# First tile of a fused attention and two-layer MLP kernel: the clamp moves from VectorE to ScalarE, and every low half of the activation goes to VectorE

## The chip, the cores and the metric

One core of one Trainium2 chip runs the whole program. The metric is device time in microseconds (us) of one execution, and lower is better. The kernel before the change took 991.78 us (median of three runs, 990.30 to 991.88).

The engines have these names in the profile: PE is TensorE's matmul stream and PEld its weight loads, DVE is VectorE, ACT is ScalarE, POOL is GpSimd, SP is SyncE, which issues the DMAs. Each engine works through its own list of instructions in the listed order.

## The reference, cut to what matters

An attention with a decaying state (4 batches, 8 heads, 768 tokens, head size 48) gives 3072 rows of 384 values; two MLPs follow, each with an inner width of 2048. The change touches the activation of the first MLP:

```python
h = x @ w_in                       # 3072 x 384 times 384 x 2048
neg, pos = h <= -1, h >= 1
g = np.where(pos, h, np.where(neg, 0.0, (h + 1) ** 2 / 4))
x = g @ w_out                      # 2048 x 384
```

## The kernel before

The 3072 tokens are cut into 8 tiles of 384 (`TILES`). For each tile of the first MLP, `step(s)` runs over 16 slices `f` of 128 inner columns, so steps 0 to 15 are the first tile. Each product is made of three matmuls on values that are split in a high and a low half: `gemm1` (line 661) issues 9 matmuls into a PSUM tile `hp`, and `gemm2` (line 670) issues 9 into the three sums `acc`, three steps later in the program (`LAG = 3`). `hp` comes from a pool of two buffers (`ps_h`), so the `hp` of a step can start only when the last reader of the `hp` two steps before is done.

Between the two products stands the activation:

- `relu2_a`: DVE clamps `hp` to [-1, 1] (line 698), ACT squares with scale and bias (line 699).
- `relu2_b`: DVE takes the larger of that and `hp` (line 711); this is the last reader of `hp`. Then `high_g` lets ACT round it to the high half `gh` (line 692).
- `low_g` (line 686), one step later, makes the low half `gl` as the difference of the two. In the first tile the engine alternates by `LOW0`, 0 being POOL and 1 being DVE: seven of the fifteen that fall under `LOW0` are on POOL and eight on DVE. From step 16 on `LOW_E` decides.

Beside the first tile run two other streams. The weights of the first MLP arrive in 32 pieces as 64-bit numbers (`wst`, line 140, four buffers) and are converted: DVE shifts and masks (line 650, into `ct`) and merges (line 652), ACT converts the low word (line 651), POOL adds the two (line 654), ACT makes the high half `whi` (line 168), and DVE or POOL the low half `wlo` (line 177, even pieces on DVE, odd ones on POOL, from piece 10 on). The attention of the next tiles goes in windows of 128 tokens (`window`): scans on DVE (lines 433 and 435), a masked copy on DVE (line 489), the scores `sc` on PE (line 484), the split of the result into `xx` (lines 537 and 538), and loads of `rk` (line 400) that a scan waits for.

What sets the order: for steps 0 to 15 (`AUTO = 16`) a scheduler of the compiler places every instruction in its engine's list by a model of its own of the time; from step 16 on the order is that of the program (`manual_schedule`). So a change in the first tile can move anything in the lists up to step 16, and nothing behind it.

Of the kernel before, what the change touches and what calls it, by code (L numbers as in the profile page):

```python
# [9 lines left out]
F32 = mybir.dt.float32  # L10
# [3 lines left out]
AF = mybir.ActivationFunctionType  # L14
# [24 lines left out]
TN = 384  # L39
# [12 lines left out]
LO0 = 'p'  # L52
LO1 = 'dg'
PUT = 1
ALT = (0,)
ALT_N = 1
N0 = 10
PRIO = True
WTS = ('wt', 'gh', 'wt', 'gl', 'wt', 'ev')
WBS = ('wb', 't')  # L60
LOW0 = (0, 1)
XL_N = 6
F0 = 0
WP0 = 400
# [35 lines left out]
def fast_path(st, tc, rkw_t, nat, v_l, w1, w2, u, out, x2_d, w2_d, flag_i, force):  # L100
    nc = tc.nc
    one = st.enter_context(tc.tile_pool(name="one", bufs=1))
    p2 = st.enter_context(tc.tile_pool(name="p2", bufs=2))
# [80 lines left out]
    def conv_w1():  # L184
        new = to_f32(0, 2) if nconv[0] < NPC else []
        if nconv[0] <= N0:
            half.extend(new)
            new = []
        while half:
            split_w(*half.pop(0))  # L190
        half.extend(new)
# [6 lines left out]
    def add_w2():  # L198
        while puts:
            i, wf = puts.pop(0)  # L200
            nc.sync.dma_start(out=w2_d[:, i, :], in_=wf)
        while adds:
            i, t, b = adds.pop(0)
            nc.gpsimd.tensor_tensor(out=t, in0=t, in1=b, op=ALU.add)
            puts.append((i, t.bitcast(F32)))
# [3 lines left out]
    def low_w2(keep):  # L209
        while len(late) > keep:  # L210
            i, wf = late.pop(0)
            f, q = pieces[i]
            (nc.gpsimd, nc.vector)[i % 2].tensor_tensor(out=wlo[f][q], in0=wf, in1=whi[f][q].bitcast(F32), op=ALU.subtract)
            load_w(2)

    def fetch_w2():
        i = nconv[2]
        if i < NPC:
            nconv[2] += 1
            f, q = pieces[i]  # L220
            wf = staged.pop((2, i))
            nc.scalar.activation(out=whi[f][q], in_=wf, func=AF.Copy)
            late.append((i, wf))
# [11 lines left out]
    def where(s):  # L235
        if s < KF * len(TILES):
            return (0, s // KF, s % KF) + TILES[s // KF]
        s -= KF * len(TILES)
        return (1, s // KF, s % KF) + TILES2[s // KF]
# [15 lines left out]
    def evac(l, i, t0, n):  # L255
        acc = accs.pop((l, i))
        for j in range(KD if l == 0 else n // 128):
            c = n if l == 0 else DM
            ev = p2.tile([128, TN], F32, tag="ev", name="ev", bufs=3)
            if j == 1:  # L260
                nc.vector.tensor_copy(ev[:, 0:c], acc[j][:, 0:c])
            else:
                nc.scalar.activation(out=ev[:, 0:c], in_=acc[j][:, 0:c], func=AF.Copy)  # L263
            if l == 0:
                nc.sync.dma_start(out=x2_d[:, j, t0:t0 + n], in_=ev[:, 0:n])
            else:
                nc.sync.dma_start(out=out[t0 + 128 * j:t0 + 128 * (j + 1)], in_=ev[:, 0:DM])

    def step(s):
        if s < NS:  # L270
            l, i, f, t0, n = where(s)
            last = l == 0 and i == len(TILES) - 1
            slots = l == 0 and not last
            if l == 0 and f == 0:
                cur[0] = i
            if l == 0 and i == 0:
                with hooks["prio"](CP1):
                    while nconv[0] < min(NPC, 2 * f + 2 + AHEAD):
                        conv_w1()
                    if nconv[0] == NPC:  # L280
                        conv_w1()
            hp = pools["h"][s % len(pools["h"])].tile([128, 512], F32, tag="h", name="hp")
            gemm1(nc, hp, n, xh[l, i], xl[l, i], f, win, whi, wlo)
            if l == 0 and ALT[f % len(ALT)] and i < ALT_N:
                t = relu2_c(nc, p2, hp, n, (None, nc.gpsimd, nc.vector)[ALT[f % len(ALT)]])
            else:
                t = (relu2_a, swish_a)[l](nc, p2, hp, n)
        if s - 1 in gq:
            low_g((nc.gpsimd, nc.vector)[(LOW_E if s >= 16 else LOW0)[s % len(LOW_E)]], p2, gq, s - 1, where(s - 1)[4])
        if s < NS:  # L290
            if slots:
                per = KF - F0 if i == 0 else KF
                if i > 0 or f >= F0:
                    credit[0] += (TILES[i + 1][1] // W) * 8 * KF // per
                if credit[0] >= KF:
                    credit[0] -= KF
                    hooks["attn"]()

        if s >= LAG:
            pl, pi, pf, pt0, pn = where(s - LAG)  # L300
            if pf == 0:
                accs[pl, pi] = [ps_a.tile([128, 512], F32, tag=f"acc{j}", name=f"acc{j}") for j in range(KD if pl == 0 else pn // 128)]
            if pl == 0:
                gemm2(nc, accs[pl, pi], pn, gq.pop(s - LAG), pf, wout, whi, wlo)
            else:
                gemm3(nc, accs[pl, pi], gq.pop(s - LAG), pf, wout, whi, wlo)
            if pf == KF - 1:
                evac(pl, pi, pt0, pn)
            if pl == 0 and pi == len(TILES) - 1:
                low_w2(0)  # L310
                while nconv[2] < 2 * (pf + 1):
                    fetch_w2()
                if pf == KF - 1:
                    low_w2(0)
        if s < NS:
            gq[s] = (relu2_b, swish_b)[l](nc, p2, t, hp, n)
        if s < NS:
            if l == 0 and i >= 1:
                if i == 1 and f == 0:
                    for _ in range(WST):  # L320
                        load_w(1)
                add_w2()
                if f in PRE_F and nconv[1] < NPC:
                    conv_w2()
            if slots:
                while credit[0] >= KF:
                    credit[0] -= KF
                    hooks["attn"]()
            if last and f == 0:
                for _ in range(WS2):  # L330
                    load_w(2)
                load_x2(0)
            if last and f == 8:
                split_x2(0)
            if l == 1 and CHECK_LATE:
                if i == 0 and f == 0:
                    for _ in range(WCK):
                        load_w(3)
                if f % 2 and nconv[3] < NPC:
                    c = nconv[3]  # L340
                    nconv[3] += 1
                    check_w(0, c, staged.pop((3, c))[:, :, 1].bitcast(I32), AF.Sigmoid)
                    load_w(3)
            if l == 1 and i + 1 < len(TILES2):
                if f == 4:
                    load_x2(i + 1)
                if f == 12:
                    split_x2(i + 1)
# [308 lines left out]
def gemm1(nc, hp, n, xh, xl, f, win, whi, wlo):  # L657
    i = 0
    for a, b in ((whi, xh), (whi, xl), (wlo, xh)):
        for kk in range(KD):  # L660
            nc.tensor.matmul(out=hp[:, 0:n], lhsT=win(a, f, kk), rhs=b[:, kk, 0:n], start=(i == 0), stop=(i == 3 * KD - 1))  # L661
            i += 1


def gemm2(nc, acc, n, g, f, wout, whi, wlo):
    gh, gl = g
    for j in range(KD):
        i = 0
        for a, b in ((whi, gh), (whi, gl), (wlo, gh)):
            nc.tensor.matmul(out=acc[j][:, 0:n], lhsT=wout(a, f, j * 128, 128), rhs=b[:, 0:n], start=(f == 0 and i == 0), stop=(f == KF - 1 and i == 2))  # L670
            i += 1


def gemm3(nc, acc, g, f, wout, whi, wlo):
    gh, gl = g
    for j, o in enumerate(acc):
        i = 0
        for a, b in ((gh, whi), (gl, whi), (gh, wlo)):
            nc.tensor.matmul(out=o[:, 0:DM], lhsT=a[:, j * 128:(j + 1) * 128], rhs=wout(b, f, 0, DM), start=(f == 0 and i == 0), stop=(f == KF - 1 and i == 2))  # L679
            i += 1  # L680


def low_g(eng, p2, gq, f, n):
    t, gh, _ = gq[f]
    gl = p2.tile([128, TN], F32R, tag="gl", name="gl", bufs=3)
    eng.tensor_tensor(out=gl[:, 0:n], in0=t[:, 0:n], in1=gh[:, 0:n].bitcast(F32), op=ALU.subtract)  # L686
    gq[f] = gh, gl
# [15 lines left out]
def relu2_c(nc, p2, hp, n, eng):  # L703
    t = p2.tile([128, TN], F32, tag="t", name="t", bufs=3)
    nc.scalar.activation(out=t[:, 0:n], in_=hp[:, 0:n], func=AF.Relu, bias=0.5, scale=0.5)
    eng.scalar_tensor_tensor(out=t[:, 0:n], in0=t[:, 0:n], scalar=1.0, in1=t[:, 0:n], op0=ALU.min, op1=ALU.mult)
    return t


def relu2_b(nc, p2, t, hp, n):  # L710
    nc.vector.tensor_tensor(out=t[:, 0:n], in0=t[:, 0:n], in1=hp[:, 0:n], op=ALU.max)  # L711
    return high_g(nc, p2, t, n)
# [163 lines left out]
```

## Time and profile before

| what | before |
|---|---|
| time, median of 3 runs | 991.78 us |
| profiled execution, its own time | 991.68 us |
| span of the profiled execution | 990.0 us |
| PE busy, share of the span | 944.4 us, 95% |
| DVE busy | 580.2 us, 59% |
| ACT busy | 528.0 us, 53% |
| POOL busy | 389.5 us, 39% |
| chain that ended last, PE's share | 80% |

The shares are means over stages that differ. The attention and the conversion of weights fill the first 120 us, with DVE and POOL near their limit and PE with gaps; after that PE has no gaps. What a change in the first tile is worth is read in that first stretch.

### The profile page before, as it was taken

To read this page: it belongs to the slowest core of one execution; us is meant where nothing else is said; L and a number is where in the kernel's file an instruction comes from. 1 tells how busy PE (TensorE), PEld (TensorE's weight loads), DVE (VectorE), ACT (ScalarE), POOL (GpSimd) and SP (SyncE) were. 2 spreads that over 40 slices of the span, in tenths; PEclk is the share of its full clock that TensorE was granted. 3 is DMA by queue.
4 is the path that set the end of the run, shared out by engine and by line. 5 is a ranking of instruction groups with operands and counts; after the bars stand their busy time and mean duration, and the time that the engine had idled before them with its cause. 6 is when DMAs were issued, how large, how long until landed. Compare 5 with 4: busy or idle time off the path is not lost.

```text
span 990.0 us, 18582 instructions
## 1 busy us (share of the span) xinstructions
PE 944.4 (95%) x6976; PEld 906.6 (92%) x6976; DVE 580.2 (59%) x1001; ACT 528.0 (53%) x1255; POOL 389.5 (39%) x398
## 2 busy tenths in 40 slices
PE   4757999999999999999999999999999999999997
PEld 2446899999999999999999999999999999999997
DVE  6889977887878778788755743232323323232321
ACT  4666555666756667665654565545454433333332
POOL 6788744555555646447423431111111111111111
PEclk9978999999999999999999999999999999999999
DMA  9876534544645445464204442323232101010000
GB/s 240 217 206 168 164 104 112 136 112 140 183 116 155 120 130 162 118 168 105 72 17 145 128 153 57 110 64 113 65 112 65 48 1 48 1 46 4 25 1 29
DMA packets 54531, 102.90 MB, mean 104 GB/s; under 512 B 8608, under 2 KB 33696, under 8 KB 54432
## 3 DMA queue, kind: packets, MB, share of 16 engines
q1 hardware_dynamic: 54432, 101.63, 36.0%
q8 instruction: 57, 0.93, 0.4%
q14 instruction: 42, 0.34, 0.1%
HBM read 83.51 MB, written 15.73 MB: 100 GB/s over the span
## 4 chain that ended last, share of the span: by engine, by line
PE 80%; DVE 7%; DMA 4%; issue 3%; ACT 3%; POOL 1%; SPq 0%; DVEq 0%; ACTq 0%; POOLq 0%
PE hp L661 37%; PE acc L679 20%; PE acc L670 18%; DMA rk<-rkw_t 2%; PE yt L515 2%; PE kv L509 2%; PE sc L484 2%; DMA wst<-w 1%; DVE pi L433 1%; DVE rk L441 1%; DVE t L711 1%; DVE t L698 1%; DVE wlo L177 1%; DVE ct L650 1%; PE tp L479 0%
## 5 line engine op out<-in xcount | busy, mean ns | idle before, releaser
L661 PE MATMUL hp<-xx,whi 128*128 128x384 f32 x1536 | 318.0, 342 | 7.4 <-DVE t L711 5.2
L686 POOL TENSOR_TENSOR gl<-t,gh 128x384 fp32r<-128x384 f32 x128 | 136.9, 1070 | 471.3 <-ACT gh L692 443.6
L661 PEld LDWEIGHTS hp<-xx,whi 128*128 128x128 f32 x1536 | 273.2, 190 | 9.8 <-DVE t L711 5.7
L692 ACT ACTIVATE gh<-t 128x384 fp32r<-128x384 f32 x256 | 134.1, 524 | 194.8 <-DVE t L711 116.8
L722 DVE TENSOR_TENSOR t<-t,hp 128x384 f32<-128x384 f32 x128 | 70.8, 553 | 218.7 <-ACT t L717 218.2
L661 PE MATMUL hp<-xx,wlo 128*128 128x384 f32 x768 | 177.6, 340 | 0.0
L717 ACT ACTIVATE t<-hp 128x384 f32<-128x384 f32 x128 | 62.9, 491 | 145.9 <-PE hp L661 145.8
L661 PEld LDWEIGHTS hp<-xx,wlo 128*128 128x128 f32 x768 | 139.0, 189 | 0.0
L670 PE MATMUL acc<-gh,whi 128*128 128x384 f32 x384 | 130.2, 350 | 0.7 <-ACT ev L263 0.6
L670 PE MATMUL acc<-gl,whi 128*128 128x384 f32 x384 | 130.3, 339 | 0.3 <-POOL gl L686 0.3
L679 PE MATMUL acc<-wlo,gh 128*128 128x384 f32 x384 | 130.2, 339 | 0.0
L679 PE MATMUL acc<-whi,gh 128*128 128x384 f32 x384 | 129.9, 338 | 0.0
L670 PE MATMUL acc<-gh,wlo 128*128 128x384 f32 x384 | 129.6, 337 | 0.0
L679 PE MATMUL acc<-whi,gl 128*128 128x384 f32 x384 | 129.3, 337 | 0.0
L686 DVE TENSOR_TENSOR gl<-t,gh 128x384 fp32r<-128x384 f32 x128 | 80.8, 631 | 51.1 <-ACT gh L692 49.7
L699 ACT ACTIVATE t<-t 128x384 f32<-128x384 f32 x128 | 66.5, 519 | 70.9 <-DVE t L698 70.5
L711 DVE TENSOR_TENSOR t<-t,hp 128x384 f32<-128x384 f32 x128 | 70.1, 548 | 30.5 <-ACT t L699 28.7
L698 DVE TENSOR_SCALAR t<-hp 128x384 f32<-128x384 f32 x128 | 70.3, 549 | 29.3 <-PE hp L661 29.1
L670 PEld LDWEIGHTS acc<-gh,whi 128*128 128x128 f32 x384 | 72.4, 190 | 3.6 <-ACT ev L263 1.3
L670 PEld LDWEIGHTS acc<-gl,whi 128*128 128x128 f32 x384 | 72.2, 188 | 0.7 <-POOL gl L686 0.5
L670 PEld LDWEIGHTS acc<-gh,wlo 128*128 128x128 f32 x384 | 72.1, 188 | 0.0
L679 PEld LDWEIGHTS acc<-whi,gl 128*128 128x128 f32 x384 | 72.1, 188 | 0.0
(98 smaller groups left out, 1278.9 us busy)
## 6 DMA issues: line engine op xcount, KB each, us to landing
wst<-w SPq DMA_DIRECT2D x96, 384.0 KB, 3.6
rk<-rkw_t SPq DMA_DIRECT2D x48, 288.9 KB, 6.1
rkn<-nat SPq DMA_DIRECT2D x24, 384.0 KB, 4.5
lt<-v_l SPq DMA_DIRECT2D x48, 128.0 KB, 3.0
w_d<-wt SPq DMA_DIRECT2D x32, 192.0 KB, 4.6
w2f<-w_d SPq DMA_DIRECT2D x32, 192.0 KB, 2.5
vn<-nat SPq DMA_DIRECT2D x24, 192.0 KB, 2.7
x_d<-ev SPq DMA_DIRECT2D x24, 192.0 KB, 4.2
```

The lines of the kernel that those rows point to most:

```text
L484: nc.tensor.matmul(out=sc[64 * (1 - hh):64 * (1 - hh) + 64, mc, :], lhsT=kt[p, mc, :], rhs=rt[p, mc, :], start=True, stop=True)
L509: nc.tensor.matmul(out=kv[c][64 * hh:64 * hh + D, m, :], lhsT=kn_t[q, m, 64 * hh:64 * hh + D], rhs=vn[q, m, hh, :], start=True, stop=True)
L661: nc.tensor.matmul(out=hp[:, 0:n], lhsT=win(a, f, kk), rhs=b[:, kk, 0:n], start=(i == 0), stop=(i == 3 * KD - 1))
L670: nc.tensor.matmul(out=acc[j][:, 0:n], lhsT=wout(a, f, j * 128, 128), rhs=b[:, 0:n], start=(f == 0 and i == 0), stop=(f == KF - 1 and i == 2))
L679: nc.tensor.matmul(out=o[:, 0:DM], lhsT=a[:, j * 128:(j + 1) * 128], rhs=wout(b, f, 0, DM), start=(f == 0 and i == 0), stop=(f == KF - 1 a ...
L686: eng.tensor_tensor(out=gl[:, 0:n], in0=t[:, 0:n], in1=gh[:, 0:n].bitcast(F32), op=ALU.subtract)
L692: nc.scalar.activation(out=gh[:, 0:n], in_=t[:, 0:n], func=AF.Copy)
L698: nc.vector.tensor_scalar(t[:, 0:n], hp[:, 0:n], scalar1=-1.0, scalar2=1.0, op0=ALU.max, op1=ALU.min)
L699: nc.scalar.activation(out=t[:, 0:n], in_=t[:, 0:n], func=AF.Square, bias=0.5, scale=0.5)
L711: nc.vector.tensor_tensor(out=t[:, 0:n], in0=t[:, 0:n], in1=hp[:, 0:n], op=ALU.max)
L717: nc.scalar.activation(out=t[:, 0:n], in_=hp[:, 0:n], func=AF.Sigmoid, scale=1.702)
L722: nc.vector.tensor_tensor(out=t[:, 0:n], in0=t[:, 0:n], in1=hp[:, 0:n], op=ALU.mult)
```

## The change

Two settings change. `ALT = (1,)` sends all 16 steps of the first tile through a new function, `relu2_d`, in place of `relu2_a`: ACT makes the clamp by two relus, out of PSUM and then in place, and squares in a third instruction. `LOW0 = (1, 1)` puts `gl` on DVE in every step of the first tile.

```diff
-ALT = (0,)
+ALT = (1,)
...
-LOW0 = (0, 1)
+LOW0 = (1, 1)
...
             if l == 0 and ALT[f % len(ALT)] and i < ALT_N:
-                t = relu2_c(nc, p2, hp, n, (None, nc.gpsimd, nc.vector)[ALT[f % len(ALT)]])
+                t = relu2_d(nc, p2, hp, n)
             else:
                 t = (relu2_a, swish_a)[l](nc, p2, hp, n)
...
+def relu2_d(nc, p2, hp, n):
+    t = p2.tile([128, TN], F32, tag="t", name="t", bufs=3)
+    nc.scalar.activation(out=t[:, 0:n], in_=hp[:, 0:n], func=AF.Relu, bias=0.5, scale=-0.5)
+    nc.scalar.activation(out=t[:, 0:n], in_=t[:, 0:n], func=AF.Relu, bias=1.0, scale=-1.0)
+    nc.scalar.activation(out=t[:, 0:n], in_=t[:, 0:n], func=AF.Square)
+    return t
```

In the changed file the two relus and the square are lines 712, 713 and 714, and the maximum is line 719 (711 before).

The scheduler then sets the lists anew. Up to the row ahead of the first clamp all of DVE's rows are as before. DVE's list just around the seventh maximum, the one that frees the `hp` buffer for step 8 (step `f` has the low half `wlo_0_` with the number 110 + 2f, so 132 belongs to slice 11). Before:

```order
L177 TENSOR_TENSOR wlo_0_132<-wt,whi_0_100 128x384
L652 SCALAR_TENSOR_TENSOR wt<-wst,ct 128x384
L698 TENSOR_SCALAR t<-hp 128x384
L434 RECIPROCAL seed<-pi 128x4
L650 TENSOR_SCALAR ct<-wst 128x384
L435 SCALAR_TENSOR_TENSOR pi<-rk_164,seed 128x516
L652 SCALAR_TENSOR_TENSOR wt<-wst,ct 128x384
L711 TENSOR_TENSOR t<-t,hp 128x384
L698 TENSOR_SCALAR t<-hp 128x384
```

and with the change:

```order
L177 TENSOR_TENSOR wlo_0_136<-wt,whi_0_104 128x384
L652 SCALAR_TENSOR_TENSOR wt<-wst,ct 128x384
L686 TENSOR_TENSOR gl<-t,gh 128x384
L650 TENSOR_SCALAR ct<-wst 128x384
L177 TENSOR_TENSOR wlo_0_138<-wt,whi_0_106 128x384
L652 SCALAR_TENSOR_TENSOR wt<-wst,ct 128x384
L650 TENSOR_SCALAR ct<-wst 128x384
L719 TENSOR_TENSOR t<-t,hp 128x384
L652 SCALAR_TENSOR_TENSOR wt<-wst,ct 128x384
L177 TENSOR_TENSOR wlo_0_140<-wt,whi_0_108 128x384
```

The same maximum now stands behind the low halves of slices 12, 13 and 14 (134, 136, 138), which came after it before.

PE's list where the scores `sc` begin of the last window that falls in the first tile. Before, from the end of the second product of step 6 on (`whi_0_96` is slice 9, `whi_1_91` slice 6):

```order
L670 MATMUL acc_932<-gl,whi_1_91 128x384
L670 MATMUL acc_932<-gh,wlo_1_123 128x384
L484 MATMUL sc<-rk_163 64x64 x5
L661 MATMUL hp<-xx,whi_0_96 128x384 x6
L661 MATMUL hp<-xx,wlo_0_128 128x384 x3
L670 MATMUL acc_930<-gh,whi_1_93 128x384
```

and with the change, from the end of the second product of step 3 on (`whi_0_90` is slice 6, `whi_1_85` slice 3):

```order
L670 MATMUL acc_936<-gl,whi_1_85 128x384
L670 MATMUL acc_936<-gh,wlo_1_117 128x384
L484 MATMUL sc<-rk_163 64x64 x16
L661 MATMUL hp<-xx,whi_0_90 128x384 x6
L661 MATMUL hp<-xx,wlo_0_122 128x384 x3
L670 MATMUL acc_934<-gh,whi_1_87 128x384
```

The scores of that window stood in three parts behind step 8 before; now they stand ahead of step 6. Everything else that PE has done when it comes to step 8 is the same in both lists. At step 12 they have done the same work altogether, and from step 17 on they agree row by row.

## Rows read from the trace of the kernel before

**Rows 1.** The page's 40 slices of the span: PE's busy tenths and its granted clock.
```profile
PE   4757999999999999999999999999999999999997
...
PEclk9978999999999999999999999999999999999999
```

**Rows 2.** Busy time by stretch: stretch, length, PE, PEld, DVE, ACT, POOL, clock, DMA share, GB/s.
```profile
79.40:116.60 37.20, 31.74 (x259) 27.72 (x255) 35.26 (x58) 21.93 (x50) 30.27 (x30) 0.86 0.57 152
116.68:144.12 27.44, 27.44 (x167) 26.48 (x168) 22.66 (x40) 16.86 (x37) 15.66 (x15) 0.94 0.51 136
144.12:990.00 845.88, 838.00 (x6066) 820.10 (x6065) 457.79 (x797) 442.94 (x1061) 284.35 (x286) 1.00 0.31 90
```

**Rows 3.** What PE's matmuls waited for, 117 us to the end (total, times, longest).
```profile
PE hp L661 <- DVE t L711: 1.8, 1, 1.8
PE acc L670 <- ACT ev L263: 0.6, 2, 0.4
PE fp L642 <- DVE st L640: 0.3, 1, 0.3
```

**Rows 4.** The chain that ended last, 110 to 150 us: start, length, what.
```profile
116.16 0.47 DVE t L711
...
116.68 3.18 PE hp L661 x9
...
121.66 0.49 PE sc L484 x10
...
124.46 0.60 PE sc L484 x14
...
128.43 0.38 PE sc L484 x8
```

**Rows 5.** DVE's groups, 79.4 to 134 us: busy, mean ns, idle before and releaser.
```profile
L177 DVE TENSOR_TENSOR wlo<-wt,whi 128x384 fp32r<-128x384 f32 x8 | 8.1, 1017 | 0.0
L650 DVE TENSOR_SCALAR ct<-wst 128x384 int32<-128x384 int32 x14 | 7.6, 546 | 0.0
...
L686 DVE TENSOR_TENSOR gl<-t,gh 128x384 fp32r<-128x384 f32 x6 | 7.5, 1255 | 0.0
L698 DVE TENSOR_SCALAR t<-hp 128x384 f32<-128x384 f32 x12 | 6.5, 544 | 0.2 <-PE hp L661 0.2
...
L489 DVE COPY_PREDICATED ra<-mask,sc 64x512 f32<-64x512 int32 x6 | 4.4, 742 | 0.2
L433 DVE TENSOR_TENSOR_SCAN pi<-rk,one_s 128x516 f32<-128x516 f32 x2 | 2.8, 1407 | 1.6 <-DMA rk<-rkw_t 1.6
...
L538 DVE TENSOR_TENSOR xx<-yt,xx 128x512 fp32r<-128x512 f32 x2 | 1.3, 666 | 0.0
```

**Rows 6.** DVE's timeline, single instructions: start, length, what.
```profile
79.47 0.54 DVE L698 TENSOR_SCALAR t<-hp 128x384 f32<-128x384 f32 x1
...
107.52 2.35 DVE L686 TENSOR_TENSOR gl<-t,gh 128x384 fp32r<-128x384 f32 x1
...
116.09 0.54 DVE L711 TENSOR_TENSOR t<-t,hp 128x384 f32<-128x384 f32 x1
116.55 0.54 DVE L698 TENSOR_SCALAR t<-hp 128x384 f32<-128x384 f32 x1
...
117.48 0.54 DVE L686 TENSOR_TENSOR gl<-t,gh 128x384 fp32r<-128x384 f32 x1
```

**Rows 7.** POOL's timeline beside two of those instructions.
```profile
107.48 1.00 POOL L654 TENSOR_TENSOR wt<-wt,wb 128x384 int32<-128x384 int32 x1
108.45 1.01 POOL L686 TENSOR_TENSOR gl<-t,gh 128x384 fp32r<-128x384 f32 x1
...
116.47 1.01 POOL L654 TENSOR_TENSOR wt<-wt,wb 128x384 int32<-128x384 int32 x1
```

**Rows 8.** ACT's groups: a PSUM read (the page) and the square (79.4 to 134 us).
```profile
L717 ACT ACTIVATE t<-hp 128x384 f32<-128x384 f32 x128 | 62.9, 491 | 145.9 <-PE hp L661 145.8
...
L699 ACT ACTIVATE t<-t 128x384 f32<-128x384 f32 x12 | 6.2, 518 | 11.7 <-DVE t L698 11.7
```

## The prediction

> **What bounds the kernel now.** I read the slices of the span first, then busy time by stretch, then PE's own waits, then the chain of waits. The slices show PE below nine tenths only in the first four of 40, about 99 us, with a lower clock in the third and fourth [rows 1]. The stretches say more in numbers: from 79.4 to 116.6 us PE is busy 31.74 of 37.20 us at a granted clock of 0.86, while DVE is busy 35.26; from 116.68 to 144.12 us PE is busy all the time, for eight steps, 8 to 15 [rows 2]. From 117 us to the end PE's matmuls waited 1.8 us for DVE's maximum (a wait that ends at 116.68), then 0.6 and 0.3 us [rows 3]. So from the first matmul of step 8, at 116.68 us, to the end this kernel is a queue of PE work without holes, and what delays that matmul by 1 us delays the end by nearly 1 us: at most about 0.9 us of later waiting can take it up. What starts it is shown by the chain: DVE's maximum of step 6, the seventh, which frees the `hp` buffer [rows 4]. DVE sits idle between 79.4 us and there almost only for one load, 1.6 us ahead of a scan [rows 5]. The question is therefore at what time DVE, in its new order, reaches the seventh maximum, and how much PE work is left then.
>
> **What is removed, added and moved in load.** Over the first tile DVE loses 16 clamps and takes seven subtractions from POOL; ACT gets two instructions more per step. DVE's instructions follow each other by less than their listed length: a maximum that is listed with 0.54 us starts at 116.09 and the next row at 116.55, so a step of 0.46, and I take 0.08 off every listed length [rows 6]. Sixteen clamps are 7.4 us. Seven subtractions are 3.2 us at 0.46 each, or 8.2 us at 1.17, the mean length of 1.255 less 0.08 [rows 5, 6]. In load, then, DVE gets between 4.2 us less and 0.8 us more. But load is not what PE waits for; position is.
>
> **Position: the seventh maximum.** I count DVE's rows from the point where the two lists part, at 79.47 us [rows 6], to the seventh maximum. The old list has 56 instructions there, the new one 69. The differences:
>
> - 7 clamps fewer: 7 x 0.46 = -3.2 us.
> - 6 shifts (line 650) and 5 merges (line 652) more, conversions that followed later before: 11 x 0.46 = +5.1. The merge is costed like the shift [rows 5].
> - 3 low halves of weights more: 1.017 less 0.08 is 0.94; +2.8 [rows 5].
> - 3 `gl` more: 3 x 1.17 = +3.5.
> - one pair of masked copies: 2 x 0.66 = +1.3; one split of `xx`: +0.6 [rows 5].
>
> Together +10.1 us. Three corrections follow. The scan that waited 1.6 us for its `rk` load has one more instruction of 0.46 ahead of it (three clamps fewer, four conversion rows more), so the wait shrinks by as much: -0.5. SP's list has one weight load more ahead of that `rk` load, and I leave it at nothing, because the load's issue also hangs on ACT's last use of the buffer. PE has the scores of the last window behind it when it comes to step 8, which before took 0.49, 0.60 and 0.38 us of the chain after that point [rows 4]: -1.5. Nothing else of PE's work is moved across that point.
>
> The third is contention. DVE's `gl` took 2.35 us while two POOL instructions, a sum and POOL's own `gl`, ran one after the other from 107.48 to 109.46, and 0.54 when POOL's sum from 116.47 ended as it began [rows 6, 7]. The Trainium skill (SBUF — State Buffer, Who interferes with whom) says that a VectorE instruction with two SBUF inputs and a GpSimd instruction that reads SBUF block each other for the whole instruction; the trace agrees in these two cases. By that rule alone, with POOL's subtractions gone and nothing in their place, the sum would come near the lower bound given below. Over its shortest step of 0.46 a `gl` loses 0.71 us on the mean and a low half 0.48; the new list has 6 and 7 of them ahead of the seventh maximum, 4.3 + 3.4 = 7.7 us of such loss. POOL is busy 30.27 of 37.20 us, a share of 0.81 [rows 2]. It loses 3 `gl` there, but gets the sums of the 5 conversions and about 3 low halves of odd pieces, at about 1.0 us each [rows 7]: 35.3 of 47.3 us, 0.75. So the loss falls by about 0.6 us: -0.6.
>
> **The sum** is 10.1 - 0.5 - 1.5 - 0.6 = **+7.5 us**. The profiled execution took 991.68 us, which is 0.1 under the median of 991.78; 991.7 + 7.5 = **999.2 us**.
>
> **What I cost at nothing.** The two relus: one reads PSUM like the sigmoid at 491 ns, one is in place like the square at 518 [rows 8]. They take the place of one clamp of 0.54 on DVE, so the path from `hp` to the maximum gets some 0.4 us longer. ACT is busy 21.93 of 37.20 us [rows 2] and waits 11.7 us for the clamps alone [rows 8], so its load has room. The cover is that `hp` of a step is finished long before its maximum's turn in DVE's list. After the seventh maximum that cover is PE itself: a step needs 27.44 / 8 = 3.4 us of PE [rows 2], more than the four ACT instructions of some 2.1 us. If the cover goes, the harder rival below is what it costs. The Trainium skill (ScalarE: Activation LUTs, Rules for kernel authors) advises relu, max and min on VectorE; by that rule the move is a loss of 16 x (0.491 + 0.518 - 0.544) = 7.4 us of engine time, which in this stretch lies on an engine with idle time. The function tables stay as they are: the list of ACT has no load of a table more.
>
> **Bounds.** With none of the loss on the port the sum is 8.1 - 7.7 = +0.4 us. With the three added `gl` at the longest length seen, 2.35 in place of 1.255, it is 8.1 + 3.3 = +11.4 us. I take the mean with its small relief, since POOL stays busy beside DVE in nearly the same share.
>
> **The rivals.**
>
> *Load decides (faster).* If PE is really held by when the conversions are through, and not by one maximum, then DVE's load counts, and with a freer port that is 4.2 us less: 987.5 us. It decides if the mean step of `gl` falls below 7.4 / 7 = 1.05 us and PE is released in step with the conversions. For it: DVE is never idle there except for one load [rows 5], and its last low half comes earlier in the new list. Against it: what the chain shows in front of step 8 is the maximum [rows 4], and the removed clamps of later steps stand behind it. Chance 0.07.
>
> *The port comes free (no change).* Without POOL's seven subtractions most of DVE's loss could go: between +0.4 and +2 us, 992.1 to 993.7 us, say 992.9. For it: two neighbours 10 us apart differ by 2.35 against 0.54 [rows 6]. Against: POOL's sums and low halves are still there and come earlier. Chance 0.15.
>
> *ACT's list adds waits (slower still).* In the new list the squares of `rk`, which wait for PE's scores, stand ahead of the rounding of step 4, and the `gl` of that step on DVE waits for this rounding. Everything behind it on DVE waits too, the conversions among it. A wait of that kind was 1.8 us where PE showed one [rows 3]; two of them make +3.6: 1002.8 us. For it: two more instructions per step in ACT's list. Against: ACT's idle time. Chance 0.14.
>
> **How the numbers follow.** The forecast has 0.64. The range reaches down into the case of the free port, to 993.0, and up to the bound of the long `gl`, 1003.0; it leaves out the faster rival, half of the free port and a little above, together under 0.2. About 0.2% (2.0 us) can be told from no change here. Slower by more than that is the forecast and the harder rival, 0.78; within it the free port, 0.15; faster the load rival, 0.07.
>
> **What would show it.** Right: the chain leaves DVE's maximum at about 125 us and from there is PE without holes; PE's first matmul of step 16 comes at about 151.6 in place of 144.1; PE's busy share from 79.4 to 116.6 us is lower than before, DVE's the same. ACT shows waits for PE in place of those for clamps. The mean `gl` on DVE stays near 1.1 us. Wrong: step 8 starts before 118 us, or PE waits again after it. The harder rival would show as idle time of DVE for ACT's `gh`; the free port as `gl` and low halves near 0.55 us.

## The result, and the profile after

The changed kernel takes **996.73 us** (median of 4 runs, 996.17 to 997.83), the kernel before in the same comparison 991.12 us (median of 4). The ratio is **1.0054, 95% interval 1.0039 to 1.0070**: slower, by 5.6 us between the medians. The forecast was 999.2 us in a range of 993.0 to 1003.0. The profiled execution after took 996.18 us with a span of 994.5 us, 4.5 us more than the one before (991.68 and 990.0).

The page's slices after, PE's busy tenths and its granted clock in tenths:

```profile
PE   4856899999999999999999999999999999999997
...
PEclk9868799999999999999999999999999999999999
```

The slices from the sixth on are as before; the fourth and fifth have PE at 6 and 8 tenths, where the row before has 7 and 9, and the fifth has a clock of 7 where it had 9 [rows 1]. The loss is again in the first 125 us. Busy time by stretch after (same columns as before: stretch, length, PE, PEld, DVE, ACT, POOL, clock, DMA share, GB/s):

```profile
79.40:116.60 37.20, 26.74 (x259) 23.24 (x260) 33.80 (x57) 27.65 (x67) 30.15 (x31) 0.82 0.69 185
79.40:124.00 44.60, 34.14 (x292) 30.49 (x292) 40.79 (x70) 32.98 (x79) 35.68 (x35) 0.81 0.71 184
124.50:149.20 24.70, 24.27 (x136) 23.96 (x137) 11.13 (x20) 16.61 (x34) 3.32 (x3) 1.00 0.14 44
149.20:994.50 845.30, 837.74 (x6066) 819.96 (x6064) 455.52 (x796) 443.97 (x1063) 283.43 (x286) 1.00 0.30 90
```

From 79.4 to 116.6 us PE does 5.0 us less than before, with DVE nearly as busy as it was (33.80 against 35.26) [rows 2]. The last stretch has PE's 837.74 us where before it had 838.00: behind step 16 nothing of weight has changed. So the difference lies in how late PE comes to step 16. PE's timeline after, single rows (start, length, what, in brackets the idle time before it and what ended that):

```profile
111.49 0.44 PE L670 MATMUL acc<-gl,whi 128*128 128x384 f32 x1 [2.83 <-DVE gl L686]
...
112.74 1.67 PE L484 MATMUL sc<-rk 48*64 48x64 f32 x32
115.63 2.29 PE L661 MATMUL hp<-xx,whi 128*128 128x384 f32 x6 [1.22 <-DVE t L719]
...
124.60 1.32 PE L661 MATMUL hp<-xx,whi 128*128 128x384 f32 x6 [0.43 <-DVE t L719]
```

The row at 124.60 is step 8, which began at 116.68 before [rows 4]: 7.9 us later. The 32 scores of the last window stand at 112.74, ahead of step 6 (the row at 115.63). In front of step 8 PE has waited only 0.43 us; the rest of the delay is older. Had the seventh maximum alone come sooner here, no more than that 0.43 us would have been won. What PE's matmuls waited for after, from 79.4 to 124.6 us and from 117 us to the end (total, times, longest):

```profile
PE acc L670 <- DVE gl L686: 4.3, 2, 2.8
PE hp L661 <- DVE t L719: 3.4, 2, 2.2
PE sc L484 <- DVE seed L434: 2.7, 1, 2.7
...
PE hp L661 <- DVE t L719: 0.4, 1, 0.4
PE acc L670 <- ACT ev L263: 0.4, 1, 0.4
PE acc L670 <- DVE gl L686: 0.3, 1, 0.3
PE fp L642 <- DVE st L640: 0.3, 1, 0.3
```

The same view of the kernel before, from 79.4 to 116.7 us:

```profile
PE hp L661 <- DVE t L711: 5.2, 3, 1.9
PE acc L670 <- POOL gl L686: 0.3, 1, 0.3
```

So 5.5 us of waiting became 10.4, and 0.43 more in front of step 8; every entry of the 10.4 is for DVE. The account closes from the stretches. From 79.4 us to the start of step 8, 37.28 us before and 45.20 after, PE was busy 31.74 and about 34.3 us (34.14 to 124.00 and 0.17 more) and so idle 5.5 and 10.9: of the 7.9 us, 5.4 are idle time and 2.6 are work, 1.5 of that the scores that now stand ahead and the rest is put down to the lower clock (0.81 against 0.86). From step 8 to step 16 PE then needed 24.45 us (124.60 to 149.05) in place of 27.44: it has the scores behind it, and it runs at a clock of 1.00, not 0.94. Net, step 16 begins 4.9 us later (149.05 against 144.12); from there to the end the changed kernel is 0.4 us shorter (845.45 against 845.88), which gives the 4.5 us between the spans.

DVE's groups after, 79.4 to 134 us (busy, mean ns, idle before and releaser):

```profile
L686 DVE TENSOR_TENSOR gl<-t,gh 128x384 fp32r<-128x384 f32 x10 | 8.7, 866 | 2.5 <-ACT gh L692 2.5
L650 DVE TENSOR_SCALAR ct<-wst 128x384 int32<-128x384 int32 x14 | 7.7, 551 | 0.1
...
L177 DVE TENSOR_TENSOR wlo<-wt,whi 128x384 fp32r<-128x384 f32 x8 | 6.4, 796 | 0.2 <-ACT whi L168 0.2
L719 DVE TENSOR_TENSOR t<-t,hp 128x384 f32<-128x384 f32 x10 | 5.5, 546 | 1.2 <-ACT t L714 1.1
...
L433 DVE TENSOR_TENSOR_SCAN pi<-rk,one_s 128x516 f32<-128x516 f32 x2 | 2.5, 1232 | 2.9 <-ACT wb L651 1.7 <-DMA rk<-rkw_t 1.2
```

A `gl` fell from 1255 to 866 ns and a low half from 1017 to 796, while shift and maximum kept theirs; and both scans now wait, 2.9 us in place of 1.6 [rows 5]. DVE's timeline after:

```profile
106.27 1.23 DVE L433 TENSOR_TENSOR_SCAN pi<-rk,one_s 128x516 f32<-128x516 f32 x1 [1.65 <-ACT wb L651]
...
115.03 0.54 DVE L719 TENSOR_TENSOR t<-t,hp 128x384 f32<-128x384 f32 x1
...
118.06 0.55 DVE L686 TENSOR_TENSOR gl<-t,gh 128x384 fp32r<-128x384 f32 x1
...
120.38 0.92 DVE L686 TENSOR_TENSOR gl<-t,gh 128x384 fp32r<-128x384 f32 x1
...
123.99 0.55 DVE L719 TENSOR_TENSOR t<-t,hp 128x384 f32<-128x384 f32 x1 [0.34 <-ACT t L714]
```

The seventh maximum starts at 123.99, before at 116.09 [rows 6]. The wait of the second scan is put down to a conversion on ACT, which had to do with other data. The chain of waits has the scan's own load in that place: SP's queue issued it in two parts from 98.99 us, and the second part landed at 106.15, just ahead of the scan at 106.27. The first line is from the queue's timeline, the second from the chain:

```profile
98.99 0.83 SPq L400 DMA_DIRECT2D rk<-rkw_t  x2
```

```profile
99.45 6.70 DMA rk<-rkw_t
```

DVE came to this scan at about 104.6 us, 5.6 us sooner than before (110.26), while the load was issued only 3.6 us sooner (98.99 against 102.57).

ACT's groups after, 79.4 to 134 us:

```profile
L713 ACT ACTIVATE t<-t 128x384 f32<-128x384 f32 x10 | 5.2, 516 | 0.0
L714 ACT ACTIVATE t<-t 128x384 f32<-128x384 f32 x9 | 4.6, 516 | 0.1
L712 ACT ACTIVATE t<-hp 128x384 f32<-128x384 f32 x9 | 4.4, 486 | 3.7 <-PE hp L661 3.5
```

The relus last 486 and 516 ns, and ACT waits 3.5 us for PE where it waited 11.7 us for clamps [rows 8].

### The profile page after: what moved, and what is told of

It reads as the page before. It is cut to its first block, busy times and chain, and to the rows that moved or that the text cites. A ratio compares the mean times of both kernels' runs of the same rounds, so it can differ in the third digit from the quotient of the medians.

```text
span 994.5 us, 18589 instructions
## 1 busy us (share of the span) xinstructions
PE 945.5 (95%) x6976; PEld 908.0 (91%) x6976; DVE 572.1 (58%) x992; ACT 542.2 (55%) x1287; POOL 381.4 (38%) x391
## 4 chain that ended last, share of the span: by engine, by line
PE 86%; DVE 5%; DMA 4%; issue 2%; ACT 1%; SPq 0%; POOL 0%; DVEq 0%; ACTq 0%; POOLq 0%
PE hp L661 39%; PE acc L679 20%; PE acc L670 20%; DMA rk<-rkw_t 3%; PE yt L515 2%; PE sc L484 2%; PE kv L509 2%; DMA wst<-w 1%; DVE pi L433 1%; PE tp L479 1%; DVE ct L650 1%; DMA xx<-xx 0%; DVE gl L686 0%; DVE wt L652 0%; DVE rk L441 0%
## 5 line engine op out<-in xcount | busy, mean ns | idle before, releaser
L686 POOL TENSOR_TENSOR gl<-t,gh 128x384 fp32r<-128x384 f32 x121 | 126.4, 1044 | 486.6 <-ACT gh L692 458.4
L686 DVE TENSOR_TENSOR gl<-t,gh 128x384 fp32r<-128x384 f32 x135 | 84.8, 628 | 55.4 <-ACT gh L692 54.0
L699 ACT ACTIVATE t<-t 128x384 f32<-128x384 f32 x112 | 58.2, 519 | 54.5 <-DVE t L698 54.1
L698 DVE TENSOR_SCALAR t<-hp 128x384 f32<-128x384 f32 x112 | 61.6, 550 | 28.3 <-PE hp L661 28.1
```

The lines of the kernel that those rows point to most:

```text
L698: nc.vector.tensor_scalar(t[:, 0:n], hp[:, 0:n], scalar1=-1.0, scalar2=1.0, op0=ALU.max, op1=ALU.min)
L699: nc.scalar.activation(out=t[:, 0:n], in_=t[:, 0:n], func=AF.Square, bias=0.5, scale=0.5)
```

## The experiments

Eleven kernels ran, in three comparisons; the medians of the kernel before in these were 992.19, 991.70 and 991.78 us, and each ratio is against those. Three explanations are set against each other. *Position* says that the end moves with the time at which DVE's list reaches the maximum that frees `hp` for step 8. *Load* says that it moves with the sum of DVE's work. *Latency* says that it moves with the longer path through ACT from `hp` to the maximum. Starts of steps are given from the first matmul of step 0, which itself lies anywhere from 65.7 to 69.0 us although the lists up to there are the same or nearly so.

**The change in two halves.** The first run has the clamp's part alone, the second the low half's.

```diff
-ALT = (0,)
+ALT = (1,)
 LOW0 = (0, 1)
```

> Clamp on ScalarE as in the change, gl alternating as before. Position theory (the end moves with the time at which VectorE's list reaches the maximum that frees hp for step 8): its list has 6 clamps fewer there, 10 conversion rows, 2 low halves and one split of xx more, no gl more, +3.6 us by the rows' lengths; PE has the scores behind it (-1.5): about +2 us, 993. Load theory (the end follows VectorE's total in the first tile): 16 clamps fewer, -7.4 us, 984. Latency theory (the longer path through ScalarE costs it all): +5.5 us, as the whole change.

Measured: 993.97 us, ratio 1.0024 (1.0013 to 1.0034).

```diff
 ALT = (0,)
-LOW0 = (0, 1)
+LOW0 = (1, 1)
```

> Clamp on VectorE as before, gl on VectorE in every step of the first tile. Position theory: 3 gl, one split of xx and one clamp more ahead of the maximum of step 6, one merge less: +3.3 us, scores ahead -1.5, and later maxima are behind by 4 to 5 us with little slack: +2 to +4 us, 993 to 995. Load theory: seven gl more, +6 us, 997. Latency theory: no change, 991.

Measured: **990.03 us, ratio 0.9983 (0.9972 to 0.9994)**. The clamp's half costs about 2 us, as position had it, and load and latency had not. In its trace, though, the largest wait of PE for a maximum, 3.05 us, is at step 6, and step 8 starts without one: the row that releases PE need not stay the one that was counted. The low half's part wins a little where all three had it lose or stay: a miss. Its step 8 came 49.5 and 50.8 us after step 0 (before and now), but now PE ran on from there at a granted clock of 1.00 and with the scores done, and needed 24.55 us to step 16 where before it needed 27.44. The halves don't add up: +2.4 and -1.7 thousandths would make +0.7, and the whole change has +5.4. What DVE waited for in the clamp's half alone, from 79.4 us to its seventh maximum:

```profile
DVE pi L433 <- DMA rk<-rkw_t: 2.9, 2, 1.8
```

Not a wait for ACT's squares among them.

**All low halves on POOL**, with the new clamp and with the old one.

```diff
 ALT = (1,)
-LOW0 = (1, 1)
+LOW0 = (0, 0)
```

> Clamp on ScalarE as in the change, gl on GpSimd in every step of the first tile. Position theory: the maximum that frees hp for step 8 is at the same place by the rows' lengths (+0.1 us): with the scores ahead and some acc matmuls behind, 990 to 992, unless the gl on GpSimd come late for acc. Load theory: VectorE has 16 clamps and 8 gl less, -14 us, 977. Latency theory: +5.5 us, 996.5.

Measured: 992.86 us, ratio 1.0008 (0.9998 to 1.0017).

```diff
 ALT = (0,)
-LOW0 = (0, 1)
+LOW0 = (0, 0)
```

> Clamp on VectorE as before, gl on GpSimd in every step of the first tile. Position theory: the maximum that frees hp for step 8 comes 2.7 us sooner, but PE has 9 acc matmuls (1.6 us) and some attention work less behind it: between -2 us and no change, 989 to 991, and a loss if gl comes late from GpSimd. Load theory: 8 gl less on VectorE, -7 us, 984. Latency theory: no change, 991.

Measured: 998.40 us, ratio 1.0061 (1.0048 to 1.0074). The first speaks against load, which wanted 14 us less, and against latency, which wanted 5.5 more; position had 990 to 992. The second is slower than both kernels though DVE has eight subtractions less than before: load falls again, and position as counted in rows misses too (-2 to 0). What DVE waited for in this last kernel, 79.4 to 125 us, and what PE waited for:

```profile
DVE pi L433 <- DMA rk<-rkw_t: 4.7, 2, 2.7
```

```profile
PE yt L515 <- DVE lt L521: 5.7, 1, 5.7
PE hp L661 <- DVE t L711: 5.6, 3, 2.6
PE kv L509 <- DVE xx L538: 2.2, 1, 2.2
```

Both scans wait for their loads, 4.7 us, and PE is then held 5.7 us by a row of the attention (line 521), beside 5.6 us in three waits for maxima, where the kernel before had 5.2. The row that PE waits for starts at 117.46, behind the second scan. This scan took 4.87 us, where the one of the kernel before at 110.26 us took 1.58, while POOL ran four instructions without a gap from 111.69 to 115.53 us, its own `gl` among them; it ended 1.1 us after the last of them. The 3.3 us are more than half of the 5.7. The scan, and two of the four:

```profile
111.75 4.87 DVE L433 TENSOR_TENSOR_SCAN pi<-rk,one_s 128x516 f32<-128x516 f32 x1 [2.69 <-DMA rk<-rkw_t]
```

```profile
112.64 0.99 POOL L686 TENSOR_TENSOR gl<-t,gh 128x384 fp32r<-128x384 f32 x1
...
114.54 0.99 POOL L436 TENSOR_TENSOR rkn<-rkn 128x384 f32<-128x384 f32 x1
```

In the run with the clamp's part alone the same scan took 3.13 us beside two POOL instructions. A row count at fixed durations can't see that: in these four runs it was off by about 1 us with the new clamp, by 3 with the low halves alone on DVE, and by 7 here.

**One instruction back to DVE.** This separates position from load, because DVE gets more work. The diff is against the changed kernel; below it stands `relu2_c`, which is in the file of both kernels already.

```diff
-                t = relu2_d(nc, p2, hp, n)
+                t = relu2_c(nc, p2, hp, n, nc.vector)
```

```python
def relu2_c(nc, p2, hp, n, eng):
    t = p2.tile([128, TN], F32, tag="t", name="t", bufs=3)
    nc.scalar.activation(out=t[:, 0:n], in_=hp[:, 0:n], func=AF.Relu, bias=0.5, scale=0.5)
    eng.scalar_tensor_tensor(out=t[:, 0:n], in0=t[:, 0:n], scalar=1.0, in1=t[:, 0:n], op0=ALU.min, op1=ALU.mult)
    return t
```

> The changed kernel with one instruction put back on DVE: ACT makes one relu, (h+1)/2 clipped at 0, out of PSUM, and DVE takes the smaller of it and 1 and multiplies by it; gl stays on DVE in every step. DVE then has 16 instructions of some 0.46 us more than in the changed kernel, 7.4 us, and the same subtractions. Position: in DVE's new list 7 conversions (13 down to 7 shifts, 13 to 7 merges), 3 low halves and 2 masked copies fewer stand ahead of the seventh maximum, and 7 of the added instructions more; at the changed kernel's own durations that is 9.8 us less, so step 8 starts within 2 us of where it starts in the kernel before, 116.7 us, and the time is that of the kernel before or up to 2 us less: 990 to 993 us, 4 to 6 under the changed kernel. Load: more work on a DVE that never idles can only be slower than the changed kernel, by up to 7.4 us: 997 to 1004 us. Latency (four ACT instructions between hp and maximum cost the time): two crossings between engines instead of one, so no better than the changed kernel: 996 to 998 us.

Measured: **990.84 us, ratio 0.9992 (0.9979 to 1.0006)**, 5.9 us under the changed kernel with 16 DVE instructions more. Step 8 came 50.8 us after step 0 (before 49.5, changed 57.1), step 16 76.7 (before 76.9, changed 81.6). Busy time from 79.4 to 116.6 us in this kernel:

```profile
79.40:116.60 37.20, 29.61 (x286) 25.84 (x280) 36.86 (x58) 22.35 (x51) 25.97 (x26) 0.91 0.57 151
```

DVE works 3 us more in this stretch than in the changed kernel, and PE gets 2.9 us more done: the sum of DVE's work is not what counts. The run is no test of latency, though the expectation says so: with two ACT instructions fewer and one DVE instruction more, the path from `hp` to the maximum is an instruction shorter, and the crossings are the same.

With `LOW0 = (0, 1)` beside it as a candidate:

> A candidate: one relu on ACT, the smaller and the product on DVE, and gl in turn on POOL and DVE as before. The seventh maximum stands 2.2 us earlier by the changed kernel's durations than with all gl on DVE (28.8 against 31.0), but POOL's subtractions are back beside DVE. Position alone: 988.5 to 990 us. If POOL's subtractions cost DVE what the run with the changed clamp's old form and all gl on DVE won, some 2 us: 990 to 993.

Measured: 993.41 us, ratio 1.0019 (1.0009 to 1.0030). That is 0.4 us above the range of the second alternative, in which POOL's subtractions cost DVE some 2 us; position alone is out by over 3 us. The list moves with the setting as well, so what part of the 2.6 us between the two kernels POOL's subtractions have is not shown.

**Rows ahead of the seventh maximum, and rows behind it.** Two kernels add four DVE instructions each to the changed kernel, four maxima in the first and four subtractions in the second, with the same values computed again.

```diff
+            for _ in range(4 if s == 6 else 0):
+                nc.vector.tensor_tensor(out=t[:, 0:n], in0=t[:, 0:n], in1=hp[:, 0:n], op=ALU.max)
             gq[s] = (relu2_b, swish_b)[l](nc, p2, t, hp, n)
```

> The changed kernel with step 6's maximum, the seventh, made five times (the same operands and result), so that four DVE instructions more, 4 x 0.46 = 1.8 us, stand ahead of what frees the hp buffer. Up to the seventh maximum the lists are those of the changed kernel; behind it one merge, one low half and the eighth maximum come between the copies, and PE takes step 9 ahead of step 8. Position: PE's first hp after the hole needs either the last copy, 1.8 + 0.47 + 0.75 + 0.46 = some 3.5 us later than in the changed kernel, or the eighth maximum, some 2.6 us later; the time 2 to 3.5 us over the changed kernel. Load: four more DVE instructions anywhere, 1.8 us, the same as in its partner with four more subtractions behind.

Measured: **999.95 us**, ratio 1.0081 (1.0064 to 1.0098); its six runs spread from 996.86 to 1003.24.

```diff
-    eng.tensor_tensor(out=gl[:, 0:n], in0=t[:, 0:n], in1=gh[:, 0:n].bitcast(F32), op=ALU.subtract)
+    for _ in range(2 if f in (7, 8, 9, 10) else 1):
+        eng.tensor_tensor(out=gl[:, 0:n], in0=t[:, 0:n], in1=gh[:, 0:n].bitcast(F32), op=ALU.subtract)
```

> The changed kernel with the gl of steps 7, 8, 9 and 10 made twice (same operands and result). The lists of all engines are those of the changed kernel but for the four added rows, all of them behind the seventh maximum. Position: the four rows, 0.5 to 0.9 us each, lie beside PE's work, which needs 3.1 to 3.4 us a step where DVE's rows of a step need under 2; the time within 0.7 us of the changed kernel's. Load: 2 to 3.6 us slower.

Measured: **996.75 us**, ratio 1.0057 (1.0045 to 1.0069). Four rows ahead cost 3.2 us between the medians, four behind nothing; with the spread of the first the sign is fairly safe and the size is not. DVE's rows in the first of the two, where line 317 is the added maximum and 721 the kernel's own, and PE's first matmul after them:

```profile
126.12 0.55 DVE L317 TENSOR_TENSOR t<-t,hp 128x384 f32<-128x384 f32 x1
126.59 0.55 DVE L654 SCALAR_TENSOR_TENSOR wt<-wst,ct 128x384 int32<-128x384 int32 x1
127.05 0.55 DVE L317 TENSOR_TENSOR t<-t,hp 128x384 f32<-128x384 f32 x1
127.52 0.59 DVE L177 TENSOR_TENSOR wlo<-wt,whi 128x384 fp32r<-128x384 f32 x1
128.03 0.54 DVE L317 TENSOR_TENSOR t<-t,hp 128x384 f32<-128x384 f32 x1
128.49 0.54 DVE L721 TENSOR_TENSOR t<-t,hp 128x384 f32<-128x384 f32 x1
```

```profile
129.09 2.29 PE L663 MATMUL hp<-xx,whi 128*128 128x384 f32 x6 [2.80 <-DVE t L721]
```

The eighth maximum, at 128.49, releases PE (step 9 stands ahead of step 8 in this list). PE comes out of the hole 60.1 us after step 0, 3.0 later than in the changed kernel; 2.6 was expected for that maximum. The execution shown is the slowest of the six, and 1.05 us of the 3.0 are there already at step 6 (49.18 us after step 0, 48.13 in the changed kernel), where the lists still agree. In the other kernel PE comes to step 8 as in the changed one, after the same wait of 0.43 us, 58.2 us after step 0 (57.1 there, and the added rows stand behind it in DVE's list; at step 6 the two are 0.9 apart), and from there it needs 24.46 us to step 16, where the changed kernel needs 24.45:

```profile
125.50 1.33 PE L661 MATMUL hp<-xx,whi 128*128 128x384 f32 x6 [0.43 <-DVE t L720]
```

**Half of the clamps, behind the place that counts.** Against the kernel before:

```diff
-ALT = (0,)
+ALT = (0,) * 8 + (1,) * 8
```

> The kernel before with ACT's two relus and square in steps 8 to 15 alone (half of the clamp's part of the change), gl alternating as before. Position: DVE's list is as before up to and with the eighth maximum, and PE runs without holes from step 8 on, so the time stays within 1 us of the kernel before. Load: 8 clamps fewer on DVE, 3.7 us less of its work, up to 3 us faster. Latency: the longer path from hp to the maximum in eight steps at some 0.4 us each, up to 3 us slower.

Measured: 991.90 us, ratio 1.0007 (0.9997 to 1.0017). Neither the 3.7 us of DVE's load nor the longer path shows in the time; the trace has one wait of PE more behind step 8, 1.28 us for a maximum at step 11.

**The scheduler's freedom ended at step 8.** The same line in the changed kernel and in the kernel before:

```diff
-AUTO = 16
+AUTO = 8
```

> The changed kernel with the scheduler's freedom ended at step 8 (AUTO 16 to 8), so that the rows of steps 8 to 15 stand in the order of the program and no conversion for them can be put ahead of the seventh maximum by the scheduler. Instructions and engines are those of the changed kernel. Position: the seventh maximum comes some 20 us earlier in DVE's list by the changed kernel's durations (20.1 against 40.8 us from the point where the lists part); what was deferred comes back as waits for conversions in steps 8 to 13, since the thirteenth maximum stands only 4 us earlier than in the changed kernel (46.2 against 50.2). Against the kernel before with the same setting its thirteenth maximum is 0.6 us earlier, so the two should be within 2 us of each other. Load or latency of the activation itself: the changed activation stays 4 to 6 us slower than the old one whatever the order.

> The kernel before with the same setting (AUTO 8), the partner of the changed kernel with AUTO 8. Position: the seventh maximum 11 us earlier in DVE's list, the thirteenth 4 us earlier; the time within 2 us of its partner's. Load or latency: 4 to 6 us faster than its partner.

Measured: 1000.02 us, ratio 1.0084 (1.0071 to 1.0097), and 992.25 us, ratio 1.0008 (0.9999 to 1.0017). The two are 7.8 us apart, not within 2: here position falls, and latency has the sign. What DVE waited for in the changed kernel with this setting, 79.4 to 134 us, and what PE waited for:

```profile
DVE t L719 <- ACT t L714: 8.2, 4, 3.0
```

```profile
PE hp L661 <- DVE wt L652: 12.3, 1, 12.3
```

and PE's row of the kernel before with it:

```profile
PE hp L661 <- ACT whi L168: 7.9, 1, 7.9
```

From 93 to 113 us DVE's list in the changed kernel with this setting has maxima, low halves and a pair of copies, and no conversion between them, so DVE stands still for ACT's instructions and the conversions wait behind:

```profile
113.74 0.56 DVE L650 TENSOR_SCALAR ct<-wst 128x384 int32<-128x384 int32 x1
```

```profile
109.12 0.56 DVE L650 TENSOR_SCALAR ct<-wst 128x384 int32<-128x384 int32 x1
```

The first row is this kernel's, 47.1 us after its step 0, the second that of the kernel before with the setting, 41.5 after. From 79.4 us to there DVE waited 11.5 us in the one (8.2 for squares, 2.7 for `gh`, 0.6 for PE) and 5.6 in the other, and PE's hole, now at step 11 and for a conversion, grows from 7.9 to 12.3 us. So a longer path through ACT can have a price of several us. The two kernels differ in the low halves too, and no run has the clamp's part alone with this setting. That the scheduler's order of 16 steps pays the same price another way, by putting conversions where DVE would have waited, is a reading and not shown.

## Why the prediction was right

**What bounds the kernel: held.** From step 8 on PE has no holes over 0.43 us, and four rows ahead of the seventh maximum move the end by 3.2 us, four behind it by nothing. PE does wait again after the first matmul of step 8, which I had named as a sign of being wrong, but only for 0.33 us.

**Load isn't what PE waits for: held.** Sixteen instructions more on DVE made the changed kernel 5.9 us faster, and sixteen clamps and eight subtractions fewer than in the kernel before (new clamp, all low halves on POOL) made no gain.

**The seventh maximum: right in kind, 1.3 us too large.** Forecast +9.0 (10.1 - 0.5 - 0.6). Counted like the forecast from the point where the lists part, at 79.47 us in the old trace and 79.71 in the new, the maximum starts 36.62 and 44.28 us behind that point: +7.7 (7.9 by the traces' own times). That the sum came so near is partly luck, for its terms miss on both sides. The *contention* step kept the mean of `gl` "near 1.1" us and took 0.6 us of relief. By the rows, six `gl` and seven low halves need 10.2 us in the new list, where three and four needed 8.7 in the old: +1.5, and not the 5.7 that the sum had for them (3.5 + 2.8 - 0.6). The *rk-wait* step was right for its scan, whose wait fell from 1.61 to 1.22 us (-0.5 reckoned); the weight load that I left at nothing put the issue of its load back by 0.5 us, and DVE came to it later still. But the other scan, which the sum doesn't have, now waits 1.65 us for its load. The eleven conversion rows cost 6.1 us and not 5.1, and DVE waits 0.34 us for ACT's square. Contention was thus 4.2 us too dear, and what was left out or too cheap makes up most of the rest: 9.0 - 4.2 + 1.8 + 1.0 + 0.3 = 7.9, and smaller rows take 0.2. The rule on the shared port (the Trainium skill, SBUF — State Buffer, Who interferes with whom) thus went further than I let it: the single rows of `gl` ahead of the maximum still run from 0.55 to 1.29 us, so POOL's instructions still block, but less often.

**One maximum as the only release: too narrow.** In front of step 8 PE waited 0.43 us. Its delay comes from the five waits ahead of that, two for maxima, two for `gl` and one for `seed`, 10.4 us in all, where before the waits ahead of the one at step 8 were 3.7. What holds is that DVE's list is late as a whole where PE looks at it; that it is late by as much at the seventh maximum is why the count of one row gave nearly the right delay.

**Scores ahead on PE: held.** Behind step 8 the changed kernel has none of them. The -1.5 are the rows of the kernel before (1.47 us); ahead of step 6 they took 1.67.

**What the sum lacked: the clock.** Before, PE came to step 8 after its hole and ran the first nine matmuls in 3.18 us [rows 4]; after, it comes there running, takes about 1.7 us (124.60 to 126.28), and has the slow nine at step 6 (115.63 to 118.88), at a granted clock of 0.50, the lower of its two levels (1.2 GHz):

```profile
115.63:118.88 3.25, 3.25 (x10) 3.25 (x11) 3.20 (x6) 2.74 (x8) 2.41 (x3) 0.50 0.58 169
```

Behind step 8 that gives back 1.5 us; ahead of it the rest of PE's longer work, about 1.1 us, is put down to the lower clock, inside the 7.9. So step 16 comes 7.9 - 1.5 - 1.5 = 4.9 us later where the forecast had 7.5.

**Costed at nothing: held, under its condition.** ACT's path cost the changed kernel 0.34 us ahead of the seventh maximum. The cover is conversions standing between square and maximum; where the order has none, DVE waits, 8.2 us for squares in the changed kernel with AUTO 8. The rival in which ACT's list adds waits was seen in small, 2.5 us of DVE's waits for `gh`, all of them behind the start of step 8. *Load decides* fell. *The port comes free* was right in part: 866 and 796 ns lie between the means of before and its 0.55 us.

**The tell-tales.** Step 16 came at 149.05, not 151.6. PE's share fell and DVE's nearly stayed. The mean `gl` did not stay near 1.1 us. The chain misses: it doesn't leave the seventh maximum but a `gl` 3 us later, since PE then waited 0.33 us more:

```profile
125.23 0.72 DVE wlo L177
125.95 1.30 DVE gl L686
...
127.29 1.32 PE acc L670 x6
```

I had looked at the chain's last hand-over as if all of the delay would show there; in truth it built up in the waits of the 45 us ahead. What stays open is why the scheduler put conversions ahead of the maxima; that it reckoned with the longer path through ACT fits the pair with AUTO 8 and the run with one instruction back on DVE, but wasn't tried by itself. Open too is how far position reaches as a rule: it missed with the low halves alone, with all of them on POOL, and with AUTO 8. Slightly better than both kernels is the old clamp with all low halves on DVE, 0.9983 of the time before.

## What to carry to other kernels

Where one engine paces another through an ordered list, count the rows ahead of the instructions that release it, of all of them and not of one, at the durations that they will have beside their new neighbours. The engine's total load can point the other way, as here, where more work on DVE made the kernel faster. The count stays blind to waits for loads and to rows that another engine lengthens, and missed by up to 7 us for it. A latency that looks covered is covered by the order, and an order that is made anew can take the cover away. And test with rows that change no value: four of them ahead of the releasing row in one kernel, four behind it in another, tell position from load.

## What was not expected of the hardware

The start of step 0 differs by up to 3.3 us between kernels (65.70 to 68.96), though their lists to there are nearly the same: it waits for a load, and differences of 1 us in later starts mean nothing unless taken from there. Even so, kernels with the same lists came to step 6 up to 1.05 us apart, counted from step 0. Nine matmuls of `hp` took 3.25 us at step 6 of the changed kernel, at a clock of 0.50 behind waits of 2.83 and 1.22 us within 7 us, and 1.6 us where PE ran on at a clock of 1.00, so which step stands behind a hole can be worth 1.6 us by itself. It is not so behind every hole: with the low halves alone on DVE, PE ran on at 1.00 behind a wait of 1.51 us. One and the same `gl` on DVE took from 0.55 to 1.37 us after and up to 2.35 before, and one and the same scan 1.23 to 4.87 us, the long ones beside POOL instructions that ran without a gap.
